# Decay attention in front of two feed-forward layers: scores and state products in four 64x64 quarters of the array, in two PSUM banks that stay one tile each

## Chip, core and metric

One Trainium2 chip, one NeuronCore of it. The metric is the device time of one execution in microseconds (us), median of the runs shown. TensorE (PE in the rows) multiplies matrices and writes to PSUM, eight banks of 128 partitions by 512 fp32 words; PEld is its loading of weights. VectorE (DVE), ScalarE (ACT) and GpSimd (POOL) do the elementwise work, SyncE (SP) issues most DMAs. Each engine takes its instructions in the order of its list and waits where a semaphore says so.

## Reference

```python
# 4 sequences, 8 heads, 768 steps, head size 48
for t in range(S):
    cur = np.einsum('bhd,bhe->bhde', u[None] * kt, vt)
    y[:, :, t] = np.einsum('bhd,bhde->bhe', rt, state + cur)
    state = w[None, :, :, None] * state + np.einsum('bhd,bhe->bhde', kt, vt)
# x = y as 3072 tokens of 384 channels
x = (np.maximum(x @ w1_in, 0.0) ** 2) @ w1_out       # 384 -> 2048 -> 384
h = x @ w2_in
out = (h - np.tanh(h)) @ w2_out                      # 384 -> 2048 -> 384
```

All in fp32.

## The kernel before

**Attention.** The 24 tiles i are 6 chunks of 128 time steps in each of 4 sequences; tile i belongs to sequence i % 4 and chunk i // 4. Tiles 0 to 3 (no state yet) go another way, through the functions that begin with `lead_`. For tiles 4 to 23 a chunk is split into two halves of 64 steps (c in the code), and the 8 heads are 4 pairs (p) of two heads (a), head a on partitions 64a to 64a+47. For each tile:

- `att_b` (entry b of the order below) multiplies keys and decayed queries to scores: 16 matmuls, each 48 rows deep, 64 weight columns, 64 moving columns. Head a of a pair goes to the other half of the partitions, so that two matmuls at a time work on two of the four 64x64 quarters of the array. All scores of the tile `sc` fill bank 5.
- `att_m` (m) copies the scores under the causal mask `low` from PSUM into `ra`, which holds the decayed queries as well: two instructions of 64x512, one for each a.
- `att_v` (sv) multiplies keys and values to the change of the state, `pv` in bank 6: 8 matmuls (2 halves x 4 pairs; in the last chunk only 4), each over all 128 partitions with 64 weight columns, two of them at a time on the two column halves of the array. The values of a head lie in one half of the partitions of `vs` and the other half is zero at that time, so one matmul takes both heads side by side (96 moving columns).
- `att_z` (z) zeroes these halves on GpSimd, two memsets of 64x384 for each tile.
- `state_1a` (s1a) adds the decayed state and the first half's `pv`, `state_1d` (s1d) decays that and adds the second half's; `put_state` (s0p, s1p) then copies the states on ScalarE into the zero half of `vs`.
- `att_c` (y) multiplies `ra` (scores and decayed queries) with `vs` (values and state) to the output `y` in bank 7; `att_eh` (xh) and `att_el` (xl) split it into two fp32r parts on ScalarE and VectorE, and `pack` (pk) moves 16-row pieces of it with six DMAs on SP into `xt`, the input of the feed-forward layers.

**Feed-forward.** Tokens go in 6 blocks of 512 (four tiles each). For each of 16 slices f of the 2048 channels, `gemm1` (h) makes 9 matmuls of 512 columns, activations follow, `gemm2_1` 9 more (g2, g2l).

**Order.** It is written out by hand. For the first block the string `first_order` lists every step; an entry `what.i` calls the function `what` with i, for instance `sv.5 y.4 ... s1a.5 ... b.5`, and the engines' lists follow that order. In it are tiles 4 to 8, the load and conversion of the first layer's weights, and the first block of that layer. From the second block on a loop runs, and beside slices 2, 5, 8 and 11 of blocks 1 to 4 it does `att_c(i)`, then `att_v(i + 1)` and `att_b(i + 1)`: tiles 9 to 23. So y of one tile is followed by pv and sc of the next on TensorE.

**Waits.** A recording layer derives the semaphores from the tiles: an instruction that writes to a tile waits for those that read it before. A tile from a pool is given a bank by its tag, `bank(5 + n)`; the next tile of that tag waits for the last reader of the one before.

Of the kernel before, what the change touches and what calls it, by code (L numbers as in the profile page):

```python
# [25 lines left out]
def decay_attention_moe_moe_kernel(  # L26
# [895 lines left out]
    def front(n):  # L922
# [7 lines left out]
        tk.0 rk.1 fl.2 fl.0 fl.1 v.1 pr.0 pb.0 k.0 r.0 pr.1 tp.0 k.1 ub.0 lbt.0 lb.0 kn.0 lb.1 dg.0 pb.1  # L930
        lbt.1 v.0 rk.2 tp.1 tt.0 lm.0 vz.0 lm.1 pr.2 r.1 rk.3 r.2 L.4 pr.3 w.0 v.2 k.2 ly.0 kn.1 tn.0
        lc.0 dg.1 lx.0 lb.2 pb.2 lb.3 lm.2 lm.3 ar.4 lbt.2 tp.2 lst.0 vz.1 dg.2 vz.2 k.3 lb.4 ly.1 kn.2 nu.4
        lb.5 r.3 lx.1 pb.3 w.2 rd.4 lbt.3 lxl.0 tp.3 lm.5 lm.4 lc.1 c0.0 kn.3 v.3 w.1 lst.1 c1a.0 ak.4 dg.3
        lb.6 c1b.0 c1a.2 ly.2 lm.6 lb.7 c2.0 lxl.1 lc.2 lm.7 nr.4 lx.2 b.4 vz.3 c3.0 lxl.2 c1a.1 nk.4 c0.2
        lst.2 ly.3 w.4 c0.1 z.4 lx.3 c1b.1 lc.3 lst.3 lxl.3 c2.1 w.3 c0.4 s0d.4 c1b.2 c2.2 sv.4 fl.3 c3.1
        ns.4 h.0 c3.2 c1a.3 rl.0 sq.0 c1a.4 h.1 c1b.4 c0.3 h.2 hi.0 w.5 rl.1 c1b.3 g2.0 sq.1 hi.1 L.5 s1a.4
        c2.3 lo.0 s0d.6 c2.4 rl.2 sq.2 g2.1 c3.3 d.4 w.7 c3.4 h.3 c0.5 nu.5 g2l.0 lo.1 w.6 rl.3 w.8 sq.3
        ak.5 c1a.5 hi.2 h.4 hi.3 g2.2 c1b.5 nr.5 s0p.4 c2.5 s0d.5 z.5 lo.2 lo.3 c0.7 g2.3 c1a.7 c3.5 w.9
        rl.4 c0.6 h.5 L.6 sq.4 c1a.6 ar.5 hi.4 c1b.7 c1b.6 c1a.8 ns.5 c2.7 c3.7 rd.5 g2l.2 g2.4 c0.8 g2l.1
        nk.5 rl.5 c2.6 sq.5 c1b.8 g2l.3 c3.6 hi.5 c0.9 c2.8 lo.5 h.7 lo.4 h.6 c3.8 rl.6 s1d.4 rl.7 sq.6  # L940
        c1a.9 g2.5 sq.7 s1p.4 c1b.9 hi.6 m.4 nu.6 w.10 c1a.10 nr.6 c0.10 c2.9 lo.6 hi.7 w.12 h.8 sv.5 y.4
        z.6 s1a.5 w.11 b.5 g2l.4 g2.6 ns.6 xh.4 c1b.10 rl.8 c1a.12 g2.7 ar.6 d.6 d.5 c0.12 lo.7 w.13 c3.9
        sq.8 s0d.7 w.14 c1a.11 c2.10 s0p.5 g2l.5 s1p.5 c0.11 c3.10 g2l.6 c1b.11 h.9 hi.8 c2.11 c1b.12 nk.6
        c2.12 L.7 rl.9 g2.8 h.10 c3.11 lo.8 sq.9 xl.4 rl.10 c3.12 c1a.13 sq.10 w.15 ak.6 h.11 h.12 g2l.7
# [220 lines left out]
```

## Time and profile before

| | |
|---|---|
| Runs shown | 881.91, 881.8 and 883.8 us, median 881.91 |
| Profiled execution, span from first to last instruction | 879.5 us |
| TensorE busy | 871.8 us, 99% |
| VectorE, ScalarE, GpSimd busy | 619.9 (70%), 642.6 (73%), 235.9 us (27%) |
| TensorE's granted clock | full (2.4 GHz) in the whole span |

The profile gives the span of the profiled execution and no other time of it. A busy share is an average over stages that differ; the matmuls are pipelined, so what a matmul costs is read from the distance between starts and not from its own duration, which holds the way through the array too. An fp32 matmul appears as two records in the trace, an fp32r one as one.

### The profile page before, as it was taken

To read this page: it belongs to the slowest core of one execution; us is meant where nothing else is said; L and a number is where in the kernel's file an instruction comes from. 1 tells how busy PE (TensorE), PEld (TensorE's weight loads), DVE (VectorE), ACT (ScalarE), POOL (GpSimd) and SP (SyncE) were. 2 spreads that over 40 slices of the span, in tenths; PEclk is the share of its full clock that TensorE was granted. 3 is DMA by queue.
4 is the path that set the end of the run, shared out by engine and by line. 5 is a ranking of instruction groups with operands and counts; after the bars stand their busy time and mean duration, and the time that the engine had idled before them with its cause. 6 is when DMAs were issued, how large, how long until landed. Compare 5 with 4: busy or idle time off the path is not lost.

```text
span 879.5 us, 14548 instructions
## 1 busy us (share of the span) xinstructions
PE 871.8 (99%) x5455; PEld 718.6 (82%) x5455; DVE 619.9 (70%) x1009; ACT 642.6 (73%) x1192; POOL 235.9 (27%) x258
## 2 busy tenths in 40 slices
...
GB/s 272 316 223 165 98 139 60 86 63 57 110 58 81 68 72 76 58 10 153 256 216 26 73 1 1 72 1 1 73 0 1 73 1 0 73 1 1 37 1 37
DMA packets 32295, 68.30 MB, mean 78 GB/s; under 512 B 5344, under 2 KB 17760, under 8 KB 32224
## 3 DMA queue, kind: packets, MB, share of 16 engines
...
q8 instruction: 43, 0.70, 0.3%
...
## 4 chain that ended last, share of the span: by engine, by line
PE 94%; ACT 2%; DVE 2%; DMA 0%; SPq 0%; issue 0%; POOL 0%; DVEq 0%; ACTq 0%; POOLq 0%
PE h L693 43%; PE o L865 22%; PE acc L741 21%; PE sc L398 2%; PE y L497 2%; PE pv L429 1%; PE pt L280 1%; PE sc L604 1%; DVE raw L100 0%; DMA vs<-in_nat_dram 0%; PE y L639 0%; ACT vs L449 0%; DVE glo L733 0%; PE y L644 0%; ACT raw L89 0%
## 5 line engine op out<-in xcount | busy, mean ns | idle before, releaser
L693 PE MATMUL h<-xt,w 128*128 128x512 f32 x864 | 211.4, 390 | 0.3 <-issue 0.3
L693 PE MATMUL h<-xs,w 128*128 128x512 f32 x864 | 211.3, 389 | 0.0
L693 PEld LDWEIGHTS h<-xt,w 128*128 128x128 f32 x864 | 161.7, 188 | 34.8 <-DMA xt<-ys 0.7
L693 PEld LDWEIGHTS h<-xs,w 128*128 128x128 f32 x864 | 162.2, 188 | 34.0
L708 ACT ACTIVATE g<-h 128x512 f32<-128x512 f32 x96 | 57.2, 597 | 147.3 <-PE h L693 111.8
L741 PE MATMUL acc<-ghi,w 128*128 128x512 f32 x576 | 149.6, 393 | 0.0
L865 PE MATMUL o<-ghi,w 128*128 128x512 f32 x574 | 148.1, 390 | 0.0
L865 PEld LDWEIGHTS o<-ghi,w 128*128 128x128 f32 x574 | 107.4, 188 | 23.3 <-ACT ob L889 1.3
L741 PEld LDWEIGHTS acc<-ghi,w 128*128 128x128 f32 x576 | 106.7, 188 | 23.0 <-ACT ghi L716 0.4
L719 POOL TENSOR_TENSOR glo<-g,ghi 128x512 fp32r<-128x512 f32 x64 | 82.5, 1288 | 151.7 <-PE acc L741 67.4
L783 POOL TENSOR_TENSOR xs<-x2f,xs 128x512 fp32r<-128x512 f32 x18 | 24.4, 1357 | 355.3 <-DVE xs L782 355.3
L520 DVE TENSOR_TENSOR ys<-y,ys 112x128 fp32r<-112x128 f32 x20 | 5.8, 290 | 157.7 <-ACT xt L516 157.7
L805 ACT ACTIVATE th<-h 128x512 f32<-128x512 f32 x96 | 57.6, 600 | 40.9 <-DVE hy L804 40.9
L865 PE MATMUL o<-glo,w 128*128 128x512 f32 x287 | 83.2, 392 | 0.3 <-DVE glo L835 0.3
L741 PE MATMUL acc<-glo,w 128*128 128x512 f32 x288 | 82.4, 390 | 0.0
L818 DVE SCALAR_TENSOR_TENSOR hy<-q,hy 128x512 f32<-128x512 f32 x96 | 76.7, 799 | 0.1
L804 DVE SCALAR_TENSOR_TENSOR hy<-h,y 128x512 f32<-128x512 f32 x96 | 66.0, 687 | 14.1 <-ACT y L802 14.1
L823 DVE COPY_PREDICATED hy<-mask,th 128x512 f32<-128x512 uint8 x96 | 70.8, 738 | 0.1
L808 DVE TENSOR_TENSOR th<-h,th 128x512 f32<-128x512 f32 x96 | 66.2, 690 | 6.0 <-ACT th L805 0.7
L806 ACT ACTIVATE q<-y,ba 128x512 f32<-128x512 f32 x96 | 68.5, 714 | 0.0
L809 ACT ACTIVATE q<-y,bb 128x512 f32<-128x512 f32 x96 | 68.5, 713 | 0.0
L812 ACT ACTIVATE mask<-y,bm 128x512 uint8<-128x512 f32 x96 | 68.3, 711 | 0.0
(112 smaller groups left out, 1187.1 us busy)
## 6 DMA issues: line engine op xcount, KB each, us to landing
...
```

The lines of the kernel that those rows point to most:

```text
L693: nc.tensor.matmul(h, lhsT=w_in(layer, f, part, kk), rhs=x[:, xpart, kk, :], start=(n == 0), stop=(n == 3 * KK - 1),)
L719: nc.gpsimd.tensor_tensor(lo, g, hi.bitcast(F32), op=ALU.subtract)
L741: nc.tensor.matmul(acc[j][m], lhsT=w_out(1, f, part, m * 128, (m + 1) * 128), rhs=g, start=(f == 0 and n == 0), stop=(f == NF - 1 and n == 2),
L804: nc.vector.scalar_tensor_tensor(out=hy, in0=h, scalar=PK, in1=y, op0=ALU.mult, op1=ALU.mult)
L805: nc.scalar.activation(out=th, in_=h, func=AF.Tanh)
L806: nc.scalar.activation(out=q1, in_=y, func=AF.Square, bias=p2["ba"], scale=1.0)
L808: nc.vector.tensor_tensor(th, h, th, op=ALU.subtract)
L809: nc.scalar.activation(out=q2, in_=y, func=AF.Square, bias=p2["bb"], scale=1.0)
L812: nc.scalar.activation(out=mask, in_=y, func=AF.Sign, bias=p2["bm"], scale=1.0)
L818: nc.vector.scalar_tensor_tensor(out=hy, in0=q2, scalar=PD, in1=hy, op0=ALU.add, op1=ALU.mult)
L823: nc.vector.copy_predicated(hy, mask, th)
L865: nc.tensor.matmul(acc[j][m], lhsT=w, rhs=g, start=(f == 0 and n == 0), stop=n == 2 and f == (NF - 2 if m == KK - 1 and j == NB - 1 else N ...
```

## The change

Scores and state products use all four quarters of the array, each matmul 64 (or 48) rows by 64 (or 48) columns. Quarters of one row half write to one bank: `scores_states()` makes two tiles `sp`, in banks 5 and 6, once, and both are kept for all tiles of the attention; scores are in their first 256 columns, the state product in the next 192. pv becomes 16 matmuls of 48 weight and 48 moving columns in place of 8 (64 weight columns for tile 4, so that no row of the bank stays unwritten); a matmul reads only the half of `vs` that holds its head's values, so `att_z` goes, and `clear()` zeroes once the rows that y reads beside the 48 of a head. The copies under the mask become four of 64x256, the additions to the state two each (`add_states`, every second head). In `first_order` the entries z go, and m.5 stands ahead of sv.6. `att_sums` and `att_bt`, which were not called, go too.

```diff
--- before.py
+++ after.py
@@ -196,6 +196,7 @@
     def clear():
         for q in range(NV):
             pads(vs_p[q], kn_p[q % 2])
+            nc.gpsimd.memset(vs_p[q][32:64, 0, 0:DM], 0.0)
         for q in range(2):
             nc.gpsimd.memset(ra_p[q][32:64, 0], 0.0)
 
@@ -389,57 +390,57 @@
     pv_t = {}
     y_t = {}
 
+    sp_t = []
+
+    def scores_states():
+        if not sp_t:
+            sp_t.extend(pbank(TPB, a, "sp") for a in range(2))
+        return sp_t
+
     def att_b(i):
-        sc_t[i] = sc = pbank(i, 0, "sc").rearrange("p (P c t) -> p P c t", P=NP, c=2)
+        sc_t[i] = sc = [t[:, 0:NP * L].rearrange("p (P t) -> p P t", P=NP) for t in scores_states()]
         for p in range(NP):
             for c in range(2):
                 for a in range(2):
                     q = slice(64 * a, 64 * a + D)
                     nc.tensor.matmul(
-                        sc[half(a), p, c, :], lhsT=rk_t[i][q, 1, p, c * L:(c + 1) * L], rhs=ra_t[i][q, a, p, c, :],
-                        start=True, stop=True,
+                        sc[a][64 * c:64 * c + 64, p, :], lhsT=rk_t[i][q, 1, p, c * L:(c + 1) * L],
+                        rhs=ra_t[i][q, a, p, c, :], start=True, stop=True,
                     )
 
-    sum_t = {}
-
-    def att_sums(i):
-        bt = sum_t[i] = pb_t[i][:, 2 * GPS:2 * GPS + 2 * NP].rearrange("p (P a) -> p P a", a=2)
-        for p in range(NP):
-            for c in range(2):
-                nc.tensor.matmul(
-                    bt[64 * c:64 * c + 64, p, :], lhsT=pr_t[i][:, p, c * L:(c + 1) * L], rhs=ucol[:, p, :],
-                    start=True, stop=True,
-                )
-
-    def att_bt(i):
-        bt = sum_t.pop(i)
-        bt_t[i] = a2.tile([128, H], F32, tag="bt", name="bt")
-        for a in range(2):
-            for c in range(2):
-                nc.scalar.activation(out=bt_t[i][half(a), c::2], in_=bt[64 * c:64 * c + 64, :, a], func=AF.Copy)
-
-    pb_t = {}
-
     def att_v(i):
-        pb = pb_t[i] = pbank(i, 1, "pv")
-        pv_t[i] = pv = pb[:, 0:2 * GPS].rearrange("p (c P d) -> p c P d", c=2, P=NP)
+        pv_t[i] = pv = [
+            t[:, NP * L:NP * L + GPS].rearrange("p (c b d) -> p c b d", c=2, d=D) for t in scores_states()[::-1]
+        ]
+        n = 64 if i == TPB else D
         for c in range(2 if i // TPB < NCH - 1 else 1):
             for p in range(NP):
                 x = (c * NP + p) * D
-                nc.tensor.matmul(
-                    pv[p % 2 * 64:p % 2 * 64 + 64, c, p // 2 * 2:p // 2 * 2 + 2, :],
-                    lhsT=kn_t[i][:, x:x + 64], rhs=vs_t[i][:, :, x:x + D], start=True, stop=True,
-                )
+                for a in range(2):
+                    q = half(a)
+                    nc.tensor.matmul(
+                        pv[a][p % 2 * 64:p % 2 * 64 + n, c, p // 2, :],
+                        lhsT=kn_t[i][q, x:x + n], rhs=vs_t[i][q, a, x:x + D], start=True, stop=True,
+                    )
+
+    def add_states(i, c, out, src):
+        for a in range(2):
+            nc.vector.tensor_tensor(
+                by_head(out)[:, :, a], by_head(src)[:, :, a], pv_t[i][a][0:GP, c], op=ALU.add
+            )
+
+    def by_head(t):
+        return t.rearrange("p (b a) d -> p b a d", a=2)
 
     def att_m(i):
         sc = sc_t.pop(i)
         for a in range(2):
-            q = half(a)
-            nc.vector.copy_predicated(
-                ra_t[i][q, a].rearrange("p P c t -> p (P c) t"),
-                low[q, q].bitcast(U32)[:, None, :].to_broadcast([64, 2 * NP, L]),
-                sc[q].rearrange("p P c t -> p (P c) t"),
-            )
+            for c in range(2):
+                s = slice(64 * c, 64 * c + 64)
+                nc.vector.copy_predicated(
+                    ra_t[i][half(a), a, :, c, :], low[s, s].bitcast(U32)[:, None, :].to_broadcast([64, NP, L]),
+                    sc[a][s],
+                )
 
     def put_state(i, c, src):
         for a in range(2):
@@ -448,12 +449,6 @@
                 rows = src[64 * e:64 * e + D].rearrange("p (b a) d -> p a b d", a=2)
                 nc.scalar.activation(out=dst[:, e], in_=rows[:, a], func=AF.Copy)
 
-    def att_z(i):
-        if i < NTAU:
-            alloc(i)
-            for a in range(2):
-                nc.gpsimd.memset(vs_t[i][64 * a:64 * a + 64, a, 0:DM], 0.0)
-
     def decay(dst, src):
         nc.vector.tensor_tensor(dst, src, wdec.to_broadcast([GP, NP, D]), op=ALU.mult)
 
@@ -470,7 +465,7 @@
 
     def state_1a(i):
         s1_t[i] = a2.tile([GP, NP, D], F32, tag="s1", name="s1", bufs=1)
-        nc.vector.tensor_tensor(s1_t[i], dec_t.pop(i), pv_t[i][0:GP, 0], op=ALU.add)
+        add_states(i, 0, s1_t[i], dec_t.pop(i))
 
     def state_1p(i):
         put_state(i, 1, s1_t[i])
@@ -479,7 +474,7 @@
         if i // TPB < NCH - 1:
             m = st_m[i % TPB]
             decay(m, s1_t[i])
-            nc.vector.tensor_tensor(m, m, pv_t[i][0:GP, 1], op=ALU.add)
+            add_states(i, 1, m, m)
 
     def state_1(i):
         state_1a(i)
...
@@ -978,7 +971,7 @@
         "apr": att_prod, "ar": att_r0, "rd": att_rd, "ak": att_k0,
         "nk": lambda i: att_k(i, V if i < 2 * TPB else G),
         "nu": lambda i: att_u(i, G), "nr": lambda i: att_r(i, G), "ns": att_s,
-        "z": att_z, "s0p": state_0p, "s0d": state_0d, "b": att_b, "sv": att_v, "dgm": att_sums, "bt": att_bt,
+        "s0p": state_0p, "s0d": state_0d, "b": att_b, "sv": att_v,
         "d": lambda i: (att_d(i, 0), att_d(i, 1)),
         "m": att_m, "s1a": state_1a, "s1p": state_1p, "s1d": state_1d,
         "y": att_c, "xh": att_eh, "xl": att_el, "pk": pack,
@@ -1027,7 +1020,6 @@
                     att_v(i)
                     att_b(i)
                     load(i + 2)
-                    att_z(i + 2)
             for what, i in todo:
                 if what == "c":
                     att_e(i)
```

How the built order changes is shown at two places in the first block. The first is TensorE's list at tile 6 (vs_95, kn_98), y of tile 5 (ra_101, vs_97) and the scores of tile 6 (ra_100). Before:

```order
L741 MATMUL acc_642<-ghi,w_9_876 128x512
L429 MATMUL pv<-vs_95,kn_98 64x96 [waits DMAHW4_49,DMAHW5_49,DVE_49,DMAHW6_49,PE_49,Pool_49]
L429 MATMUL pv<-vs_95,kn_98 64x96 x7
L497 MATMUL y<-ra_101,vs_97 64x64 [waits DVE_49,PE_49]
L497 MATMUL y<-ra_101,vs_97 64x64 [waits DVE_49]
L497 MATMUL y<-ra_101,vs_97 64x64 x14
L398 MATMUL sc<-ra_100,rkt 64x64 [waits DMAHW4_49,DMAHW2_49,PE_49]
L398 MATMUL sc<-ra_100,rkt 64x64 [waits DMAHW5_49]
L398 MATMUL sc<-ra_100,rkt 64x64 x14
```

And with the change:

```order
L736 MATMUL acc_651<-ghi,w_9_887 128x512
L421 MATMUL sp<-vs_95,kn_98 48x48 [waits DMAHW5_49,DMAHW4_49,DVE_49]
L421 MATMUL sp<-vs_95,kn_98 48x48 [waits DMAHW6_49]
L421 MATMUL sp<-vs_95,kn_98 48x48 x14
L492 MATMUL y<-ra_101,vs_97 64x64 [waits PE_49,Pool_49]
L492 MATMUL y<-ra_101,vs_97 64x64 [waits Pool_49]
L492 MATMUL y<-ra_101,vs_97 64x64 x14
L406 MATMUL sp<-ra_100,rkt 64x64 [waits DMAHW4_49,DMAHW2_49,DVE_49]
L406 MATMUL sp<-ra_100,rkt 64x64 [waits DMAHW5_49]
L406 MATMUL sp<-ra_100,rkt 64x64 x14
```

By the semaphore's counts in the built program, DVE_49 at pv stood for s1d.5's addition before (st from pv) and stands for the last copy of m.5 now; at the scores no wait for VectorE stood before, and DVE_49 there now stands for the second addition of s1a.6. In the same way sv.5 now waits for m.4, b.5 for s1a.5, and sv.7, as before, for s1d.6.

The second place is VectorE's list around the same tile, where m.5 (the copies into ra_101) and s1a.6 (the addition s_1135, now s_1159) stand. Before:

```order
L733 TENSOR_TENSOR glo<-g,ghi 128x512 [waits PE_49]
L438 COPY_PREDICATED ra_101<-low,sc 64x512 [waits Pool_49] x2
L349 TENSOR_TENSOR rkt<-rkt,tr 112x512 [waits DMAHW7_49,DMAHW6_49,DMAHW0_49]
L120 TENSOR_TENSOR w_13_1126<-raw,w_13_1126 128x768 [waits Activation_49]
L96 TENSOR_SCALAR raw<-raw 128x768 [waits DMAHW3_49]
L317 TENSOR_REDUCE bt<-rnt 128x2x4 [waits Pool_49]
L473 TENSOR_TENSOR s_1135<-dec,pv 112x192 [waits PE_49]
```

And with the change:

```order
L728 TENSOR_TENSOR glo<-g,ghi 128x512 [waits PE_49]
L440 COPY_PREDICATED ra_101<-low,sp 64x4x64 [waits Pool_49]
L440 COPY_PREDICATED ra_101<-low,sp 64x4x64
L440 COPY_PREDICATED ra_101<-low,sp 64x4x64 [waits Pool_49]
L440 COPY_PREDICATED ra_101<-low,sp 64x4x64
L350 TENSOR_TENSOR rkt<-rkt,tr 112x512 [waits DMAHW7_49,DMAHW6_49,DMAHW0_49]
L120 TENSOR_TENSOR w_13_1150<-raw,w_13_1150 128x768 [waits Activation_49]
L96 TENSOR_SCALAR raw<-raw 128x768 [waits DMAHW3_49]
L318 TENSOR_REDUCE bt<-rnt 128x2x4 [waits Pool_49]
L428 TENSOR_TENSOR s_1159<-dec,sp 112x2x48 [waits PE_49] x2
```

Nothing has moved past anything else here; four steps of other work stand between m.5 and s1a.6 as before, and TensorE's scores of tile 6 now wait for what stands behind them.

## Rows read from the trace of the kernel before

**Rows 1.** Busy us (instructions) of each engine in two stretches; granted clock, DMA.
```profile
core 0: us, PE busy (x) PEld busy (x) DVE busy (x) ACT busy (x) POOL busy (x), PEclk, DMA share, GB/s
30.00:60.00 30.00, 29.99 (x145) 23.96 (x143) 29.38 (x41) 26.45 (x46) 11.63 (x10) 1.00 0.82 287
240.00:325.00 85.00, 85.00 (x651) 70.28 (x651) 27.08 (x52) 44.62 (x96) 45.27 (x49) 1.00 0.22 69
```
**Rows 2.** Timeline of TensorE, steady part: start, us to the last end, tile, records.
```profile
123.85 1.15 PE L497 MATMUL y<-ra,vs 128*64 128x64 f32 x32
124.83 0.83 PE L429 MATMUL pv<-vs,kn 128*64 128x96 f32 x16
125.59 1.15 PE L398 MATMUL sc<-ra,rkt 48*64 48x64 f32 x32
126.67 0.96 PE L741 MATMUL acc<-ghi,w 128*128 128x512 f32 x3
...
325.68 0.50 PE L429 MATMUL pv<-vs,kn 128*64 128x96 f32 x8
```
**Rows 3.** Timeline of TensorE, 8 to 25 us: lead_b, and a cut block of scores.
```profile
9.31 1.10 PE L604 MATMUL sc<-first 48*64 48x128 f32 x32
...
14.30 0.67 PE L604 MATMUL sc<-first 48*64 48x128 f32 x16
...
24.63 0.56 PE L398 MATMUL sc<-ra,rkt 48*64 48x64 f32 x12
```
**Rows 4.** Groups by line: shapes, count | busy us, mean ns of one | idle before.
```profile
L657 PEld LDWEIGHTS pt<-first_v,first_kn 128*64 128x64 f32 x64 | 2.3, 137 | 0.3 <-issue 0.2
L644 PEld LDWEIGHTS y<-am,first_v 128*48 128x48 f32 x48 | 2.9, 123 | 0.0
L455 POOL MEMSET vs<- 64x384 f32 x40 | 17.4, 434 | 7.1 <-PE y L497 6.1
L615 DVE COPY_PREDICATED am<-low,sc 128x256 f32<-128x256 uint32 x16 | 6.0, 441 | 1.4 <-POOL am L327 1.2 <-PE sc L604 0.2
```
**Rows 5.** Timeline of VectorE, 24 to 112 us.
```profile
24.73 0.77 DVE L615 COPY_PREDICATED am<-low,sc 128x256 f32<-128x256 uint32 x2
...
58.68 1.51 DVE L438 COPY_PREDICATED ra<-low,sc 64x512 f32<-64x512 uint32 x2
...
90.07 0.35 DVE L482 TENSOR_TENSOR st<-st,pv 112x192 f32<-112x192 f32 x1
90.34 0.28 DVE L520 TENSOR_TENSOR ys<-y,ys 112x128 fp32r<-112x128 f32 x1
90.54 0.55 DVE L520 TENSOR_TENSOR xt<-y,xt 112x384 fp32r<-112x384 f32 x1
```
**Rows 6.** Timelines of TensorE and VectorE around tile 5.
```profile
59.20 0.88 PE L429 MATMUL pv<-vs,kn 128*64 128x96 f32 x16
61.32 1.15 PE L398 MATMUL sc<-ra,rkt 48*64 48x64 f32 x32
...
68.30 2.71 DVE L100 SCALAR_TENSOR_TENSOR raw<-raw 128x768 uint32<-128x768 uint32 x2 [1.33 <-ACT raw L89]
```
**Rows 7.** Timeline of all engines around tile 6; in brackets idle time and its releaser.
```profile
79.98 1.52 DVE L438 COPY_PREDICATED ra<-low,sc 64x512 f32<-64x512 uint32 x2
80.31 0.88 PE L429 MATMUL pv<-vs,kn 128*64 128x96 f32 x16
82.63 1.15 PE L398 MATMUL sc<-ra,rkt 48*64 48x64 f32 x32
84.03 0.34 DVE L473 TENSOR_TENSOR s<-dec,pv 112x192 f32<-112x192 f32 x1
90.63 0.88 PE L429 MATMUL pv<-vs,kn 128*64 128x96 f32 x16 [0.49 <-DMA vs<-in_nat_dram]
```
**Rows 8.** Timelines of SP's queue and TensorE at the end of the first block.
```profile
91.15 3.92 SPq L532 DMA_DIRECT2D xt<-ys  x6
...
97.97 8.93 SPq L532 DMA_DIRECT2D xt<-ys  x12
...
108.24 3.44 PE L693 MATMUL h<-xt,w 128*128 128x512 f32 x14 [0.34 <-issue]
```

More of the change, by code (lines that the diff above doesn't have):

```diff
@@ L929, in decay_attention_moe_moe_kernel @@
     first_order = """
[L930 to L944, printed above, removed]
@@ L945, in decay_attention_moe_moe_kernel @@
-        s1d.5 hi.10 nu.7 hi.9 g2.10 lo.9 c0.13 c1b.13 rl.11 lo.10 sq.11 g2.9 sv.6 z.7 m.5 ar.7 c0.14 c2.13
-        c3.13 c1a.15 nr.7 rd.6 ns.7 s1a.6 y.5 rl.12 sq.12 c1a.14 b.6 hi.11 lo.11 s0p.6 ak.7 c0.15 h.13 s1p.6
-        pk.4 rd.7 xh.5 g2l.8 c1b.15 g2.11 c1b.14 m.6 hi.12 nk.7 c2.14 g2.12 g2l.10 c2.15 s1d.6 xl.5 sv.7 L.8 pk.5
-        z.8 y.6 c3.15 s1a.7 c3.14 nu.8 d.7 b.7 z.9 h.14 nr.8 L.9 s1p.7 xh.6 ak.8 g2l.9 s0d.8 rl.13 xl.6 pk.6
-        s0p.7 m.7 sq.13 h.15 nk.8 lo.12 s0d.9 s1d.7 ar.8 rl.14 sq.14 g2l.11 y.7 sv.8 nu.9 ns.8
@@ L950, in decay_attention_moe_moe_kernel @@
-        hi.14 hi.13 xh.7 xl.7 b.8 nr.9 lo.13 rl.15 s1a.8 ar.9 pk.7 g2.13 sq.15 nk.9 g2.14 g2l.12 hi.15 lo.14
-        ns.9 lo.15 g2l.13 s0p.8 g2l.14 z.10 h.16 s1d.8 rl.16 sq.16 h.17 g2b.15 hi.16 ak.9 rl.17 ev.1 sq.17
-        hi.17 g2a.15 g2c.15 ev.0 L.10 d.8 d.9 ev.2 m.8 s1p.8
+        tk.0 rk.1 fl.2 fl.0 fl.1 v.1 pr.0 pb.0 k.0 r.0 pr.1 tp.0 k.1 ub.0 lbt.0 lb.0 kn.0 lb.1 dg.0 pb.1 lbt.1 v.0
+        rk.2 tp.1 tt.0 lm.0 vz.0 lm.1 pr.2 r.1 rk.3 r.2 L.4 pr.3 w.0 v.2 k.2 ly.0 kn.1 tn.0 lc.0 dg.1 lx.0 lb.2 pb.2
@@ new lines, in decay_attention_moe_moe_kernel @@
+        lb.3 lm.2 lm.3 ar.4 lbt.2 tp.2 lst.0 vz.1 dg.2 vz.2 k.3 lb.4 ly.1 kn.2 nu.4 lb.5 r.3 lx.1 pb.3 w.2 rd.4 lbt.3
+        lxl.0 tp.3 lm.5 lm.4 lc.1 c0.0 kn.3 v.3 w.1 lst.1 c1a.0 ak.4 dg.3 lb.6 c1b.0 c1a.2 ly.2 lm.6 lb.7 c2.0 lxl.1
+        lc.2 lm.7 nr.4 lx.2 b.4 vz.3 c3.0 lxl.2 c1a.1 nk.4 c0.2 lst.2 ly.3 w.4 c0.1 lx.3 c1b.1 lc.3 lst.3 lxl.3 c2.1
+        w.3 c0.4 s0d.4 c1b.2 c2.2 sv.4 fl.3 c3.1 ns.4 h.0 c3.2 c1a.3 rl.0 sq.0 c1a.4 h.1 c1b.4 c0.3 h.2 hi.0 w.5 rl.1
+        c1b.3 g2.0 sq.1 hi.1 L.5 s1a.4 c2.3 lo.0 s0d.6 c2.4 rl.2 sq.2 g2.1 c3.3 d.4 w.7 c3.4 h.3 c0.5 nu.5 g2l.0 lo.1
@@ new lines, in decay_attention_moe_moe_kernel @@
+        w.6 rl.3 w.8 sq.3 ak.5 c1a.5 hi.2 h.4 hi.3 g2.2 c1b.5 nr.5 s0p.4 c2.5 s0d.5 lo.2 lo.3 c0.7 g2.3 c1a.7 c3.5 w.9
+        rl.4 c0.6 h.5 L.6 sq.4 c1a.6 ar.5 hi.4 c1b.7 c1b.6 c1a.8 ns.5 c2.7 c3.7 rd.5 g2l.2 g2.4 c0.8 g2l.1 nk.5 rl.5
+        c2.6 sq.5 c1b.8 g2l.3 c3.6 hi.5 c0.9 c2.8 lo.5 h.7 lo.4 h.6 c3.8 rl.6 s1d.4 rl.7 sq.6 c1a.9 g2.5 sq.7 s1p.4
+        c1b.9 hi.6 m.4 nu.6 w.10 c1a.10 nr.6 c0.10 c2.9 lo.6 hi.7 w.12 h.8 sv.5 y.4 s1a.5 w.11 b.5 g2l.4 g2.6 ns.6
+        xh.4 c1b.10 rl.8 c1a.12 g2.7 ar.6 d.6 d.5 c0.12 lo.7 w.13 c3.9 sq.8 s0d.7 w.14 c1a.11 c2.10 s0p.5 g2l.5 s1p.5
```

9 lines of the change are left out of this document (added).

## The prediction

> **What bounds the kernel now.** I read the busy time by stretches first [rows 1]: TensorE is busy without a gap from 240 to 325 us, at the full granted clock, while VectorE, ScalarE and GpSimd are at 32%, 52% and 53% of that stretch. It is the same in every stretch from 110 us on, so from there a microsecond taken from TensorE is one taken from the end. From 30 to 60 us it is otherwise: TensorE and VectorE are both full (29.99 and 29.38 of 30), and the list `first_order` has woven them together; there a gain of one engine counts only where the other isn't waited for.
>
> Then the timeline of TensorE shows what one attention tile costs it [rows 2]. In the steady part a tile is y, pv, sc in a row: from 123.85 to 126.67, 2.82 us. pv takes 0.76 of it, sc 1.08. Each fp32 matmul appears as two records: 32 records are the 16 matmuls of sc, 16 are the 8 of pv.
>
> **What a record costs.** Differences of rows free the cost of a record from entry and tail. pv: 0.83 for 16 records, 0.50 for the 8 of a tile of the last chunk, so 0.33/8 = 41 ns. sc: 1.15 for 32, 0.56 for its first 12 in another tile, so 0.59/20 = 29 ns [rows 2, 3]. Both work on two parts of the array at once, so a pair takes 82 and 58 ns. The kernel already has one place with four quarters and a bank per row half: `lead_b`, 1.10 for 32 records and 0.67 for 16, so 0.43/16 = 27 ns for records of 128 moving columns [rows 3]. Four of them take 108 ns: twice the columns of sc, and yet less per record.
>
> **sc.** The same 32 records, now in 8 groups of four. A group is between 54 ns (half of the 108, for half the columns) and 58 (what a pair of this shape takes). I take 58, since four loads of 64 weight columns have to fit in as well: 8 x 0.058 = 0.465 in place of 32 x 0.029 = 0.93. Saved: 0.465.
>
> **pv.** The 8 matmuls of 128 rows by 96 columns become 16 of 64 rows by 48: 32 records, 8 groups. The bounds of a group: 41 ns (108 x 48/128) and 58 (if what the 64-column pair takes were a floor). Which one binds is read from the weight loads: 123 ns where 48 columns are loaded, 137 where 64 are [rows 4]. 14 ns less than 58 is 44; I take 45. 8 x 0.045 = 0.36 in place of 16 x 0.041 = 0.66. Saved: 0.30, or 0.20 at the upper bound.
>
> The change of the array's division, which costs sc its entry now (the 1.08 hold some 0.15 over 0.93), moves to the entry of pv and isn't paid twice in the steady order y, pv, sc.
>
> **Steady sum.** Tiles 9 to 19 have two state products: 11 x 0.765 = 8.4 us. Tiles 20 to 23 have one: 4 x (0.465 + 0.15) = 2.5. Together 10.9 us; 9.5 at the upper bound of pv.
>
> **GpSimd.** 40 memsets at 434 ns, 17.4 us, are gone [rows 4], and three of 32x384 stand at the start. I cost both at nothing: GpSimd has half of each steady stretch free. If the three were not hidden, they would cost at most 3 x 0.43 at the start.
>
> **VectorE.** A tile's two copies under the mask become four of half the size, each of its two state additions two. What an instruction occupies is the distance to the next start. Two copies of 64x512 are 1.51 from the first start to the last end; two of 128x256 are 0.77, of which the second starts 0.33 after the first, since one alone takes 0.44 [rows 4, 5]. Four of 64x256 are then 1.32 at 0.33 each, 1.54 as twice the 0.77, and 1.76 if each took its full 0.44: between -0.2 and +0.24 a tile. I take +0.06. An addition of 192 elements occupies 0.27 (90.07 to 90.34), 128 elements 0.20 (90.34 to 90.54) [rows 5], so 96 some 0.17: two are 0.34, +0.07 an addition; at most +0.17. In the steady part that is 0.2 us of an engine that idles two thirds of the time. Before 110 us it counts.
>
> **The first stage, tiles 4 to 8.** Here the kept tile matters more than the quarters. pv and sc of a tile now share two banks, and the rows of the order show the price: sv.6 waits for the last copy of m.5, b.6 for the last addition of s1a.6, waits that were not there (b waited for m, sv for s1d). Queued behind them on TensorE is all of the feed-forward work. I follow the chain.
> - Tile 5 [rows 5, 6]. m.4 ends at 60.19 (58.68 + 1.51); with two split additions ahead of it and its own +0.06 at 60.4. sv.5 starts there and not at 59.20. With 0.5 for pv and its entry, and y.4's 1.1 with its change of division, b.5 starts near 61.95 (61.32 before) and, being shorter, ends at 62.55 (61.32 + 1.08 = 62.40 before): +0.15. s1a.5 is done by then. What ScalarE takes from y.4 comes some 0.3 later, in its turn, and VectorE, which stood 1.33 us for ScalarE until 68.30, goes on there 0.3 later; that wait swallows VectorE's own additions up to then.
> - Tile 6 [rows 7]. m.5 ends at 81.50, now 0.3 + 0.07 + 0.06 later: 81.93. sv.6 moves from 80.31 to there, y.5 runs to 83.6. b.6 then waits for s1a.6, which stands four VectorE steps behind m.5, at 84.03 before, 84.46 now, done at 84.9. b.6 ends at 85.5 (82.63 + 1.08 = 83.71 before): +1.8.
> - Tiles 7 and 8. At sv.7 TensorE had 0.49 us of waiting (90.63; the row names a DMA, but the built order ties sv.7 to VectorE's s1d.6, 90.07 + 0.35), so it comes there +1.3. y, pv and sc of tile 7 are shorter by 0.6, those of tile 8 by 0.77: +0.7, then -0.1.
> - What ends the stage is another queue [rows 8]: SP issues the DMAs that pack x, with the next tile's loads between them, from 91.15 to 106.90 (97.97 + 8.93), and the first h of the next block starts behind them at 108.24. SP's chain starts when xl.5 is done on VectorE (90.54 + 0.55 [rows 5]), and that comes later by 0.3 and by the splits of s1d.5, m.5, s1a.6, m.6, s1d.6 (0.07 + 0.06 + 0.07 + 0.06 + 0.07): +0.6 us. So TensorE waits longer at 108 whatever it gained, and the stage ends 0.6 us later, not earlier. With each split at its upper bound (0.17 and 0.24) and 0.7 instead of 0.3 it is +1.7; with copies at the lower bound it is nothing.
>
> **Sum.** -10.9 + 0.6 = -10.3 us. The profiled span goes from 879.5 to 869.2. The median of the runs shown, 881.91, lies 2.4 above that span, which I carry unchanged: 871.6 us.
>
> **Rivals.**
> 1. *Four records don't go in the time of two.* No row has a mean under 27 ns per record, neither pairs nor quarters. If 27 to 29 ns were a floor of the instruction stream, sc would stay at 0.87 to 0.93 and pv, with its records doubled, would go from 0.66 to 0.87 to 0.93: +0.14 to +0.27 a tile, 2 to 3.5 us over the steady tiles, 1 us in the first stage: 884.5 to 886.5, slower. It decides at 1.59/64 = 24.8 ns a record: above it the steady part loses. For it: that all shapes with 64 weight columns, from 2 to 64 moving columns, come at 58 ns a pair. Against it: the time of `lead_b` is explained by its columns, and weight loads that differ by 16 columns differ by 15 ns, so the 58 looks like the load. The Trainium skill (TensorE: Matmul & The Clock Gate, "Wait — 56ns, not 53.3ns?") puts such a floor at about 25 ns from start to start however few the columns, and TensorEngine Tiling (Array Packing), "Instruction Overhead", warns against splitting a dimension that is already small. By that 25, an estimate from the page, 64 records are 1.60 us against 1.59 now: no change. The trace neither shows a mean below it nor an end that only it explains. Chance 0.07 for slower, 0.05 for within the bound.
> 2. *The first stage keeps its gain.* If the new waits found their work done, five tiles would bring 5 x 0.765 less three extra changes of division at 0.15: 3.4 us, 867.6. Against it stands SP's chain, which TensorE can't shorten. Chance 0.08.
> 3. *The first stage loses more*: both waits of tile 6 fall later since a load or a GpSimd mask slips with them, 3 to 6 us in place of 0.6, so 874 to 878. Chance 0.10.
>
> My forecast, 870.5 to 874.1 by its own bounds (9.5 with +1.7 at one end), has 0.70. The range 868.5 to 875.5 takes in most of rival 2 and the near end of rival 3, and leaves out some 2 in 10. What a measurement can tell from no change is about 0.3%, 2.6 us. Faster 0.88, same 0.05, slower 0.07.
>
> **What the profile after should show.** sc rows of 32 records at 0.69 in place of 1.15, pv rows of 32 at 0.45 or so in place of 0.83 with 16, y to the next acc at 2.06 in place of 2.82. A copy at 0.42 to 0.45, an addition at 0.26. Waits of pv and sc for VectorE at about 60, 82 and 84 us, and the first h of the second block near 108.9. If sc is still near 1.1 or pv over 0.8, rival 1 holds; if the second block starts after 112, rival 3.

## The result, and the profile after

The changed kernel takes 872.8 us (median; 872.15 to 873.04), the kernel before 881.86 beside it: a ratio of 0.9896, 95% interval 0.9882 to 0.991, 9.1 us less. The forecast was 871.6, in a range of 868.5 to 875.5. The profiled span is 870.4 us, again 2.4 below the median.

The page of the changed kernel: busy time, then the chain that ended last.

```profile
span 870.4 us, 15121 instructions
...
PE 858.7 (99%) x5743; PEld 705.1 (81%) x5743; DVE 642.6 (74%) x1085; ACT 643.2 (74%) x1192; POOL 222.9 (26%) x221
...
PE 91%; DVE 6%; ACT 1%; issue 1%; DMA 0%; SPq 0%; POOL 0%; DVEq 0%; ACTq 0%; POOLq 0%
```

TensorE has 13.1 us less to do, VectorE 22.7 more. Busy time by the two stretches of [rows 1]:

```profile
30.00:60.00 30.00, 29.13 (x125) 22.86 (x124) 29.35 (x45) 26.43 (x46) 9.89 (x6) 1.00 0.82 284
240.00:325.00 85.00, 85.00 (x790) 69.98 (x789) 37.00 (x75) 48.11 (x107) 46.26 (x43) 1.00 0.26 81
```

In the steady part TensorE is still the only full engine. Before, 30 to 60 us had it busy for 29.99; it now stands 0.87 us while VectorE is as full as before: the first sign of where something was lost. TensorE's timeline in the steady part, to be laid beside [rows 2]:

```profile
125.09 1.15 PE L492 MATMUL y<-ra,vs 128*64 128x64 f32 x32
126.17 0.58 PE L421 MATMUL sp<-vs,kn 64*48 64x48 f32 x32
126.57 0.66 PE L406 MATMUL sp<-ra,rkt 48*64 48x64 f32 x32
127.16 1.21 PE L736 MATMUL acc<-ghi,w 128*128 128x512 f32 x4
...
319.12 0.40 PE L421 MATMUL sp<-vs,kn 64*48 64x48 f32 x16
```

y to the next acc is 2.07 us in place of 2.82. pv, with twice the records, falls from 0.76 to 0.40, sc from 1.08 to 0.59. y grows by 0.10: the change of the array's division, from halves of 64 columns to quarters, now stands behind it. The two hybrids below differ in this at y.7: 1.10 us to the next start where quarters follow, 0.98 where they don't.

The groups by line (count | busy us, mean ns) show the weight loads and VectorE's halves:

```profile
L406 PEld LDWEIGHTS sp<-ra,rkt 48*64 48x64 f32 x640 | 11.3, 135 | 2.0 <-DVE s L428 1.9
L421 PEld LDWEIGHTS sp<-vs,kn 64*48 64x48 f32 (+1 forms) x576 | 8.6, 122 | 5.2 <-DVE ra L440 3.0 <-DVE st L428 0.8 <-DVE kn L310 0.3
L440 DVE COPY_PREDICATED ra<-low,sp 64x256 f32<-64x256 uint32 x80 | 35.7, 446 | 4.8 <-POOL ra L328 2.7
L428 DVE TENSOR_TENSOR s<-dec,sp 112x96 f32<-112x96 f32 x40 | 8.2, 246 | 0.1
```

The first stage, timelines of VectorE, TensorE and SP's queue (compare [rows 5 to 8]):

```profile
58.60 1.81 DVE L440 COPY_PREDICATED ra<-low,sp 64x256 f32<-64x256 uint32 x4
60.44 0.56 DVE L96 TENSOR_SCALAR raw<-raw 128x768 uint32<-128x768 uint32 x1
60.47 0.57 PE L421 MATMUL sp<-vs,kn 64*48 64x48 f32 x32 [1.33 <-DVE ra L440]
...
81.57 0.57 PE L421 MATMUL sp<-vs,kn 64*48 64x48 f32 x32 [0.87 <-DVE ra L440]
84.55 0.69 PE L406 MATMUL sp<-ra,rkt 48*64 48x64 f32 x32 [1.32 <-DVE s L428]
...
87.94 1.85 DVE L440 COPY_PREDICATED ra<-low,sp 64x256 f32<-64x256 uint32 x4
89.82 1.07 DVE L310 TENSOR_TENSOR kn<-kn,kt_tab 128x384 f32<-128x384 f32 x1
90.81 0.80 DVE L453 TENSOR_TENSOR st<-s,wst 112x192 f32<-112x192 f32 x1
91.64 0.42 DVE L428 TENSOR_TENSOR st<-st,sp 112x96 f32<-112x96 f32 x2
92.79 4.36 SPq L527 DMA_DIRECT2D xt<-ys  x6
100.04 8.11 SPq L527 DMA_DIRECT2D xt<-ys  x12
107.47 0.97 PE L736 MATMUL acc<-glo,w 128*128 128x512 f32 x3 [0.36 <-DVE glo L728]
108.27 4.65 PE L688 MATMUL h<-xt,w 128*128 128x512 f32 x18
109.48 3.44 PE L688 MATMUL h<-xt,w 128*128 128x512 f32 x14
```

The last line shows the same 18 matmuls from the fifth on, as the last of [rows 8] does. The rows of the kernel before that stand against some of these, then GpSimd's row there and its first two now:

```profile
60.10 0.54 DVE L96 TENSOR_SCALAR raw<-raw 128x768 uint32<-128x768 uint32 x1
...
87.81 1.52 DVE L438 COPY_PREDICATED ra<-low,sc 64x512 f32<-64x512 uint32 x2
89.23 0.53 DVE L309 TENSOR_TENSOR kn<-kn,kt_tab 128x384 f32<-128x384 f32 x1
89.69 0.34 DVE L458 TENSOR_TENSOR st<-s,wst 112x192 f32<-112x192 f32 x1
89.77 1.12 POOL L301 TENSOR_TENSOR rnt<-rnt,ub 128x384 f32<-128x384 f32 x1 [5.34 <-DVE kn L309]
```

```profile
89.46 1.01 POOL L302 TENSOR_TENSOR rnt<-rnt,ub 128x384 f32<-128x384 f32 x1 [13.61 <-DMA rnt<-in_nat_dram]
90.55 1.58 POOL L328 TENSOR_SCALAR_AFFINE_SELECT ra<-bt 64x512 f32<-64x512 f32 x2
```

The forecast waits are there, at 60.5, 81.6 and 84.6 us. y.8, the first step of the second block that belongs to attention, starts at 125.09 in place of 123.85, 1.24 later. From it to the last y it is 266.84 us, before 277.07. So the steady part brought 10.23 us and the first stage took back 1.24.

The trace also settles what ends the first stage. The fifth h of the second block starts 0.09 us behind the landing of SP's last pack DMA, in both kernels (108.24 behind 108.15 before, 109.48 behind 109.39 now), and y.8 starts 15.70 behind that landing in both.

### The profile page after: what moved, and what is told of

The parts are those of the page before. It is cut to its first block, busy times and chain, and to the rows that moved or that the text cites. A ratio compares the mean times of both kernels' runs of the same rounds, so it can differ in the third digit from the quotient of the medians.

```text
span 870.4 us, 15121 instructions
## 1 busy us (share of the span) xinstructions
PE 858.7 (99%) x5743; PEld 705.1 (81%) x5743; DVE 642.6 (74%) x1085; ACT 643.2 (74%) x1192; POOL 222.9 (26%) x221
## 4 chain that ended last, share of the span: by engine, by line
PE 91%; DVE 6%; ACT 1%; issue 1%; DMA 0%; SPq 0%; POOL 0%; DVEq 0%; ACTq 0%; POOLq 0%
PE h L688 42%; PE o L860 22%; PE acc L736 20%; PE y L492 2%; DVE raw L100 1%; DVE w L120 1%; PE sp L406 1%; PE sp L421 1%; DVE glo L728 1%; PE pt L281 1%; DVE ra L440 1%; PE sc L599 0%; DVE raw L96 0%; DMA kn<-in_nat_dram 0%; PE pk L566 0%
## 5 line engine op out<-in xcount | busy, mean ns | idle before, releaser
L714 POOL TENSOR_TENSOR glo<-g,ghi 128x512 fp32r<-128x512 f32 x64 | 87.8, 1371 | 147.3 <-PE acc L736 78.1
```

What stands on the lines that cost most here:

```text
L714: nc.gpsimd.tensor_tensor(lo, g, hi.bitcast(F32), op=ALU.subtract)
```

## Experiments

A first question was how far two executions of one kernel differ; each run left one profile. Of the kernels in the changed form, those whose first scores start near 24.5 us have y.8 at 125.09, 125.67 and 126.03; the others start at 25.2 to 26.0 with the same instructions up to there, and have y.8 at 125.87 to 129.65. From y.8 on the profiles repeat to 0.01 us. Steady differences are therefore read from y.8 to the last y, and the first stage by where y.8 falls.

**Are four quarters at once the gain? Scores two and two.**

```diff
-        for p in range(NP):
-            for c in range(2):
+        for c in range(2):
+            for p in range(NP):
                 for a in range(2):
```

> The changed kernel, but the 16 score matmuls of a tile are issued with the half c outermost, so that only two quarters (the two row halves of one column half) are at work at a time; nothing else differs. Theory (the gain of sc comes from four quarters working at once): a pair takes the 58 ns that a group of four takes now, so sc goes from 8 x 58 ns to 16 x 58 ns, +0.465 us a tile, 15 x 0.465 = +7.0 us in the steady part and up to +2.3 in the first stage: 879.8 to 882.1 us, sc from start to next 1.05 us. Rival (the gain comes from something else that the change brought, as a bank for each row half or the saved change of division): sc stays at 0.59, time 872.5 to 873.1 us.

Measured: 879.21 us, ratio 0.9954 (0.9938 to 0.997); sc from start to next 0.88, y.8 to the last y 270.30 us, +3.46. The rival is out, but the theory's +7.0 is halved. The starts of the 32 records in the trace say why (ns behind the first):

```
changed kernel  0 7 14 20 | 72 79 85 92 | 130 137 144 150 | 189 ... 422 429 435 442
two and two     0 7 | 72 79 | 130 137 | 189 195 | 247 254 | 266 273 | 305 312 | 364 370 | 373 380 | 422 429 | 431 438 | 490 ... 723 730
before          0 7 | 107 113 | 165 172 | 223 230 | 282 288 | 340 ... 923 930
```

Four records come every 58 ns in the changed kernel, two before. With c outermost it begins with pairs; after five of them a second series starts at 266, while the first goes on at 305, 364, 422 with the six records that it has left. The rows don't name the half of a record; by the order of issue the second series is the second column half, which then didn't wait for the first to be issued to its end. So the block is 266 + 464 long and not twice as long.

The median is 6.4 us above the changed kernel. Three of the seven executions took 876.26 to 876.66, about what the steady part alone adds; four took 879.21 to 880.22. The profiled one is the longest of these, and loses 4.56 us ahead of y.8 (129.65), of which 1.5 were there at the first scores. Behind a wait of TensorE the clock fell. First TensorE's timeline, then windows of 2 us, with the granted clock in the third last place:

```profile
105.89 0.97 PE L406 MATMUL sp<-ra,rkt 48*64 48x64 f32 x30 [1.08 <-DVE ra L354]
106.78 4.56 PE L736 MATMUL acc<-ghi,w 128*128 128x512 f32 x12
```

```profile
104.00:106.00 2.00, 0.54 (x14) 0.30 (x7) 1.94 (x3) 1.56 (x4) 1.92 (x2) 1.00 0.15 32
106.00:108.00 2.00, 2.00 (x33) 1.74 (x34) 2.00 (x7) 0.23 (x1) 0.69 (x1) 0.68 0.05 9
108.00:110.00 2.00, 2.00 (x7) 1.52 (x6) 1.97 (x5) 1.92 (x5) 0.00 (x0) 0.50 0.12 25
```

TensorE was busy for 0.54 of 2 us, then got 0.50, the lower of its two levels (1.2 of 2.4 GHz); the 12 matmuls of acc took 4.56 in place of 3.01. The hybrid with Q = 8, further below, has waits of 0.18 and 1.09 us at the same place (here 0.38 and 1.08) and kept 1.00. So the clock doesn't fall there in every profile, which may be what parts the executions into two groups; that wasn't tried.

**State products two and two.**

```diff
-            for p in range(NP):
-                x = (c * NP + p) * D
-                for a in range(2):
+            for a in range(2):
+                for p in range(NP):
+                    x = (c * NP + p) * D
```

> The changed kernel, but the state products are issued with the row half a outermost, so that only the two column halves of one row half are at work at a time; nothing else differs. Theory (four 48x48 matmuls share one period of 45 ns because they are in four quarters): a pair takes 45 ns, so pv goes from 8 x 45 to 16 x 45 ns, +0.36 us a tile with two products and +0.18 with one: 11 x 0.36 + 4 x 0.18 = +4.7 us, up to +1.8 more in the first stage: 877.5 to 879.3 us. Rival (it is the 48 weight columns and 48 moving columns that made pv short, and a pair needs only 22 to 25 ns): pv stays near 0.40, 872.5 to 873.3 us.

Measured: 874.15 us, ratio 0.9907 (0.9889 to 0.9924); pv 0.40 as in the changed kernel, y.8 to the last y 267.18, +0.34. By the numbers the rival's outcome. Yet the rows don't show pairs at 22 ns:

```profile
127.83 0.56 PE L421 MATMUL sp<-vs,kn 64*48 64x48 f32 x30
128.22 0.23 PE L406 MATMUL sp<-ra,rkt 48*64 48x64 f32 x1
128.22 0.21 PE L421 MATMUL sp<-vs,kn 64*48 64x48 f32 x2
128.24 0.68 PE L406 MATMUL sp<-ra,rkt 48*64 48x64 f32 x31
```

A record of the scores, which stand behind the state products in the program, starts ahead of the last two of these. And inside pv the starts are 0 7 27 33 | 80 87 107 113 | 125 132 152 158 | 170 ...: four in 45 ns, though four matmuls of one row half are issued ahead of the other's. By that pattern TensorE had started the other half past six records that were waiting. The same would explain e1, and it could be put to a test with a number.

**All of one row half first.**

```diff
-        for c in range(2 if i // TPB < NCH - 1 else 1):
-            for p in range(NP):
-                x = (c * NP + p) * D
-                for a in range(2):
+        for a in range(2):
+            for c in range(2 if i // TPB < NCH - 1 else 1):
+                for p in range(NP):
+                    x = (c * NP + p) * D
```

> The changed kernel, but all state products of one row half (8 matmuls, 16 records) are issued before those of the other, where e2 issued them 4 and 4 and still had groups of four. Theory (TensorE starts a record for a free quarter ahead of some 6 records that wait for busy ones, as in e1, where the other column half started with 6 records of the first still to come): the second row half starts about 4 x 45 + 20 = 200 ns after the first, pv goes from 0.40 to 0.60 us, tile to tile +0.1 to +0.2 us, with one product a tile no change to what e2 showed (0.215). Rival 1 (a pair needs only 22 ns): pv stays at 0.40. Rival 2 (it looks ahead over the whole product): 0.40 with groups of four, as in e2. Time 873 to 875.5 by the theory, 872.2 to 874 by the rivals; the rows decide.

Measured: 875.1 us, ratio 0.992 (0.9907 to 0.9932); starts 0 7 | 80 87 | 125 132 | 170 177 | 215 222 | **228 235** | 260 267 | 305 308 312 315 ... 578 585. The second half starts at 228, with ten records gone and six to come, pv is some 0.59 (0.228 + 8 x 0.045), and y.8 to the last y 269.16, +2.3 or 0.21 a tile of two products. Both rivals are out. It is four quarters that make pv short, and TensorE finds them by itself past waiting records: in all three runs the other half started with six records of the first still to come.

**Does the weight load set the 45 ns?** All state products load 64 columns:

```diff
-        n = 64 if i == TPB else D
+        n = 64
```

> The changed kernel, but all state products load 64 weight columns in place of 48 (the 16 more give rows that nothing reads). Theory (the period of a group of four is that of its weight load, 45 ns with 48 columns, 58 with 64): 8 groups x 13 ns, pv +0.10 us a tile with two products, +0.05 with one, 11 x 0.104 + 4 x 0.052 = +1.35 us in the steady part, period of tile to tile 14.68 in place of 14.573. Rival (the moving columns, 48 in both, set the period): pv stays at 0.396, no difference to the control beyond 0.5 us.

Measured: 875.04 us, ratio 0.9924 (0.991 to 0.9937); starts 0 7 13 20 | 94 101 107 114 | 152 159 166 172 | 211 ..., a group in 58 ns; pv 0.50, tile to tile 14.68, y.8 to the last y 268.23: +1.39 for the forecast 1.35. The moving columns, 48 in both, don't set it. The period goes with the weight columns, and the loads of the changed kernel themselves differ by the same 13 ns (121 for 48 columns, 134 for the 64 of tile 4).

**VectorE's splits alone,** in the kernel before:

```diff
         for a in range(2):
             q = half(a)
-            nc.vector.copy_predicated(
+            for c in range(2):
+                nc.vector.copy_predicated(
...
-        nc.vector.tensor_tensor(s1_t[i], dec_t.pop(i), pv_t[i][0:GP, 0], op=ALU.add)
+        add_states(i, 0, s1_t[i], dec_t.pop(i))
```

> The kernel before, with only VectorE's part of the change: four copies of 64x256 under the mask in place of two of 64x512, and two additions of 96 elements in place of one of 192. TensorE's work, banks and waits are those of before, apart from the split. Theory A (the first stage lost through the waits of the tile that is kept, its end is set by TensorE and SP): 0.44 us more of VectorE a tile, most of it in idle time, xl.5 comes some 0.4 later and SP's chain with it: 882.0 to 882.5 us. Theory B (from 60 to 108 us VectorE itself is the bound, and what the splits add there is added to the end): 5 tiles x 0.44, +1.5 to +2.2 us: 883.4 to 884.1 us. In both nothing is lost after 110 us.

Measured: 882.75 us, ratio 1.0007 (0.9997 to 1.0017); y.8 at 123.74, y.8 to the last y 277.07, both as before. SP's pack DMAs start at 91.61, 0.46 later than in [rows 8]. That is theory A's number, but not its cause alone: here too kn took 1.17 and the decay 0.80 (0.53 and 0.34 before) beside a GpSimd step that began at 88.26, ahead of kn. SP's DMAs then ran shorter, and TensorE reaches the second block in time all the same. Theory B's 1.5 to 2.2 us are not there in the profile, which is of the shortest of ten executions. The median leaves up to 1.5 open.

**Same work, other order on VectorE.**

```diff
-        ... sq.6 c1a.9 ... hi.6 m.4 nu.6 ... c1b.13 rl.11 lo.10 sq.11 g2.9
-        m.5 sv.6 ar.7 c0.14 ... ns.7 s1a.6 y.5
+        ... sq.6 m.4 c1a.9 ... hi.6 nu.6 ... c1b.13 m.5 rl.11 lo.10 sq.11 g2.9
+        sv.6 ar.7 s1a.6 c0.14 ... ns.7 y.5
```

> The changed kernel with three entries of the written order moved on VectorE: m.4 ahead of the two shift steps it stood behind (1.6 us earlier), m.5 ahead of the low part lo.10 (0.7 us earlier), s1a.6 directly behind ar.7 (1.9 us earlier). No engine gets other work. It takes away most of the waits of TensorE for VectorE at 60.5, 81.6 and 84.6 us (1.33, 0.87 and 1.32 us). Theory A (these waits are the loss of the first stage): the second block starts 1 to 2 us earlier, until SP's chain or the last low part holds it: 870.8 to 871.9 us. Theory B (VectorE is full until the stage ends, and work only changes places on it): the second block starts at 108.3 as now, 872.5 to 873.1 us.

Measured: 873.94 us, ratio 0.9905 (0.9889 to 0.9921); y.8 at 127.44, with first scores 0.8 later than in the profile after. The waits at 60 and 82 us are gone (0 and 0.18), that of b.6 too, but b.5 now waits 1.38 for s1a.5, and at sv.7:

```profile
91.41 1.77 DVE L453 TENSOR_TENSOR st<-s,wst 112x192 f32<-112x192 f32 x1
...
93.52 0.73 PE L421 MATMUL sp<-vs,kn 64*48 64x48 f32 x32 [2.56 <-DVE st L428]
94.44 1.97 PE L492 MATMUL y<-ra,vs 128*64 128x64 f32 x32 [0.19 <-PE sp L421]
```

The decay step, 0.34 us before, took 1.77 beside GpSimd's masks and products (90.4 to 94.0), and behind TensorE's wait the clock was 0.62 from 94 to 96 us, so that y took 1.97. The run doesn't separate the theories as meant: the waits changed place, and one of them grew for another reason.

**GpSimd kept quiet there.**

```diff
-        sv.7 L.8 pk.5 y.6 c3.15 s1a.7 c3.14 nu.8 d.7 b.7 h.14 nr.8 L.9 ...
-        s0p.7 m.7 sq.13 h.15 nk.8 lo.12 ...
+        sv.7 L.8 pk.5 y.6 c3.15 s1a.7 c3.14 d.7 b.7 h.14 L.9 ...
+        s0p.7 m.7 sq.13 h.15 lo.12 ...
```

> The changed kernel without three GpSimd steps of tile 8 (nu.8, nr.8, nk.8: the products with u, with the keys and with the key table are left out), which ran on GpSimd from 89.5 to 94.8 us, while VectorE's steps took 1.07 in place of 0.53 us (kn), 0.80 in place of 0.35 (decay) and 1.27 and 1.42 in place of 0.95 (low parts). Theory (VectorE is slowed by GpSimd there and TensorE's pv.7 waits for VectorE): VectorE reaches s1d.6 0.9 us earlier, pv.7's wait of 0.36 goes, the stage ends 0.4 to 1.3 us earlier. Rival (VectorE is slowed by something else, or the stage's end does not hang on it): the same durations of VectorE and no difference to the control beyond 0.4 us.

The kernel leaves out three GpSimd steps of tile 8, so its output isn't the reference's.

Measured: 873.5 us, ratio 0.9909 (0.9896 to 0.9923), no different from the control (873.12, below).

```profile
84.70 0.84 DVE L96 TENSOR_SCALAR raw<-raw 128x768 uint32<-128x768 uint32 x1
85.47 1.12 DVE L728 TENSOR_TENSOR glo<-g,ghi 128x512 fp32r<-128x512 f32 x1
...
90.83 0.56 DVE L310 TENSOR_TENSOR kn<-kn,kt_tab 128x384 f32<-128x384 f32 x1
91.31 0.35 DVE L453 TENSOR_TENSOR st<-s,wst 112x192 f32<-112x192 f32 x1
...
92.84 4.68 SPq L527 DMA_DIRECT2D xt<-ys  x6
```

kn and the decay are back at 0.56 and 0.35: GpSimd is what slowed them. But its masks of tile 7, no longer behind nu.8, now ran at 84.47, and there two other steps took 0.84 and 1.12 (0.56 and 0.69 in the profile after). SP's chain starts at 92.84, where the changed kernel has 92.79. The overlap moved, and nothing was won.

**The control, and the old form in the first stage only.** The hybrid takes the old form in each of the four functions (in `add_states` by a branch inside it), as in

```diff
+    Q = 2 * TPB
...
     def att_b(i):
+        if i < Q:
+            return pair_b(i)
```

with the bodies of the kernel before behind it, and keeps that kernel's order and z for the tiles below Q.

> The changed kernel, unedited, on the same chip as the next three, so that they have a median to stand against. Its first record of scores fell between 24.5 and 26.0 us in the profiles of kernels that differ only later, so executions differ by about a microsecond before tile 5: 872.2 to 874.5 us, y of tile 8 at 125 to 127 us.

> Tiles 4 to 7 in the form and the order of the kernel before (pairs, two banks of their own, two copies, one addition, z memsets), tiles 8 to 23 in the changed form. Theory A (in the first stage the changed form itself costs: waits of TensorE on the kept tile and split VectorE work, about 1.4 us from the first scores to y.8): y.8 comes 99.2 us after the first scores as in the kernel before (123.85 - 24.63) in place of 100.6 (125.09 - 24.47), the steady part is as in the changed kernel: 1.0 to 1.8 us below the control. Rival (the loss is not from the form, but from where loads and SP's pack chain happened to fall): y.8 as far behind the first scores as in the control, time within 0.5 us of it.

> As the hybrid of e6, but tile 8 too keeps the form of the kernel before; the changed form starts with tile 9, so the written order of the first stage is that of the kernel before. Theory A (the changed form is what costs in the first stage): y.8 comes 99.2 us after the first scores, as in the kernel before, steady part as in the changed kernel (266.84 us from y.8 to the last y, plus up to 0.1 for the first product of 64 columns): 871.0 to 872.5 us, within 0.5 of e6 and 0.7 to 1.8 below the control. Rival (e6 won by the shorter TensorE work of tile 8, or by chance): 872.6 to 873.5 us, with y.8 at 100.5 or more behind the first scores.

Measured: control 873.12 us, ratio 0.9907 (0.9893 to 0.992), y.8 at 126.03; hybrid with Q = 8, on the same chip, 871.89, ratio 0.9889 (0.9875 to 0.9902), y.8 at 124.28; with Q = 9, in another run, 872.08, ratio 0.9898 (0.9881 to 0.9916), y.8 at 124.32, with two of its six executions at 874.39 and 876.26. y.8 to the last y is 266.84, 266.84 and 266.95. Control, then hybrid (Q = 8), timelines of TensorE and SP:

```profile
107.85 0.96 PE L736 MATMUL acc<-glo,w 128*128 128x512 f32 x3 [0.75 <-DVE glo L728]
108.65 1.20 PE L688 MATMUL h<-xt,w 128*128 128x512 f32 x4
110.42 3.44 PE L688 MATMUL h<-xt,w 128*128 128x512 f32 x14 [0.57 <-issue]
...
100.76 8.33 SPq L527 DMA_DIRECT2D xt<-ys  x12
```

```profile
107.85 4.26 PE L735 MATMUL h<-xt,w 128*128 128x512 f32 x18
...
90.86 3.93 SPq L574 DMA_DIRECT2D xt<-ys  x6
...
97.68 9.66 SPq L574 DMA_DIRECT2D xt<-ys  x12
```

In the control TensorE does four matmuls of the second block and stands for SP, whose last pack DMA was issued at 109.09 (100.76 + 8.33). In the hybrid SP is done at 107.34 and TensorE goes straight through.

By the yardstick that was set, y.8 behind the first scores, Q = 8 with 99.72 is nearer to the theory's 99.2, but Q = 9 with 100.35 is nearer to the rival's 100.5: e10 decides nothing by it. What ends the stage, SP's chain, gives a better one. Its first DMA behind xl.5 starts 66.3 to 67.4 us behind the first scores in the four profiles with the old form on TensorE there (before, e6, e10, and e3 with VectorE's splits), and 68.0 to 69.1 in all eight of the changed form and its variants. How long the DMAs then take differs between executions of one kernel: in the profile after and the control, which run the same kernel, the chain starts at 92.79; its last DMA lands 16.60 us later in the first and 17.54 in the second, where two issues took 1.74 and 1.17 (at most 0.95 in the first, 0.59 for most). That is the whole 0.94 between their y.8.

So theory A holds in direction: the changed form starts SP's chain later, and y.8 stands at 125.09 to 126.03 in the three profiles that start near 24.5 us, at 123.74 to 124.32 in the four of the old form. The size, 1 to 2 us, rests on one profile of each run. The hybrid has the lowest median of all, but the intervals of its ratio and the control's overlap.

## Why the prediction came out as it did

- *sc, 58 ns a group of four*: right. 8 groups at 58, block 0.49 shorter (forecast 0.465).
- *pv, 45 ns, set by the load of 48 columns*: right, and shown by e7, where 64 columns gave 58. The block is 0.37 shorter (forecast 0.30).
- *The change of division, not paid twice*: right. pv and sc together are 0.855 shorter and y is 0.10 longer, so 0.755 in all for the forecast 0.765.
- *Steady sum, -10.9*: -10.23 measured. Of the missing 0.67, 0.16 lie in the blocks (0.754 for 0.765 and 0.605 for 0.615). The rest, 0.034 a tile, lies behind them: tile to tile went from 15.293 to 14.573, 0.720 and not 0.754. The first ten matmuls of acc and h behind the scores take some 35 ns longer together than before. What slows them wasn't tried.
- *GpSimd's memsets at nothing*: right. GpSimd's busy time fell from 235.9 to 222.9. In the steady part ScalarE waits 30.1 us in all for its masks and VectorE 2.7, the same before and after, and no wait of TensorE shows there.
- *Four copies, +0.06 a tile, bounds -0.2 to +0.24*: mis-sized, and outside its bounds. From the first start to the next step it is 1.84 (58.60 to 60.44) in place of 1.42 (58.68 to 60.10), +0.42. A copy of 64x256 occupies its 0.45 whole; the step of 0.33 that [rows 5] showed for 128x256 didn't carry over. The additions are as taken (0.34 for 0.27).
- *First stage, +0.6, bounds 0 to 1.7*: right in its mechanism, too small in size: +1.24 in the profile after, some +2.2 in the control. The three waits came at their places, for m.4, m.5 and s1a.6. The chain through xl.5 to SP's DMAs is the one forecast, but they start at 92.79, 1.64 behind 91.15 and not 0.6. From start to start, by the rows of the section on the result, m.6 begins 0.13 later, its four copies cost 0.46 more, kn 0.53, the decay 0.45, the additions 0.07. So 0.98 of 1.64 are kn and decay beside GpSimd, which I hadn't on the list. In the kernel before, GpSimd's step began at 89.77, behind the start of kn and of the decay; now it began at 89.46, ahead of both. That 1.64 lies inside the bounds is luck: they were made of slips and splits. And that only 1.24 of it reached y.8 is luck as well: SP's DMAs took 16.60 us to the last landing in place of 17.00. In the control, with 17.54, it is 2.18.
- *What ends the stage*: right, SP. The 108.24 that the prediction calls the first h is the fifth matmul of the block. Held against 109.48 it came 1.24 later, as y.8 did. The wait for VectorE's low parts at 107.47 (0.36) stands ahead of that and sets nothing, since the fifth h waits for the landing all the same.
- *Rival 1, a floor per record*: out. Four records in 58 and 45 ns are 14.5 and 11.3 ns each. The Trainium skill's start-to-start floor of about 25 ns (TensorE: Matmul & The Clock Gate, "Wait — 56ns, not 53.3ns?") doesn't hold across quarters: the rows have starts 6 to 7 ns apart.
- *Rivals 2 and 3*: the first stage kept nothing, and lost 1 to 2 us, not 3 to 6. e1 and e4 show how a loss like that of rival 3 can come about: one longer wait, and then the lower clock.

The two errors have one sign: 0.7 less gained, 0.6 more lost, about the distance from 871.6 to 872.8.
